# Attention and a gated layer on one core: the last output tile cut at column 448 instead of 384

## The chip, the cores and the metric

The kernel runs on one core of a Trainium2 chip. The metric is the device time of one execution in microseconds; lower is better. Three runs of the kernel before gave 247.82, 247.95 and 248.65 us, median 247.95.

Engines are named as in the profile: PE is the matrix engine (TensorE), with PEld its weight loads; DVE the vector engine; ACT the scalar engine; POOL and SP the two others, which here only move data. A q behind a name (SPq, ACTq) means the instructions with which that engine starts a DMA or waits.

## The reference

For each of 8 batches and 8 heads (576 tokens, head size 64) two attentions follow each other: 32 packed queries p attend to k and v, and the packed result serves as keys and values for q. The heads are joined to rows of 512, and a two-layer network with a gated activation follows:

```python
def sm_attn(qq, kk, vv):
    s = scale * np.matmul(qq, kk.transpose(0, 1, 3, 2))
    a = np.exp(s - np.max(s, axis=-1, keepdims=True))
    return np.matmul(a / (np.sum(a, axis=-1, keepdims=True) + 1e-09), vv)

p_packed = sm_attn(p, k, v)
x = sm_attn(q, p_packed, p_packed)       # heads joined: 4608 x 512
h = x @ w_in                             # 4608 x 2048
g = np.where(h >= 1, h, np.where(h <= -1, 0.0, (h + 1) ** 2 / 4))
out = g @ w_out                          # 4608 x 512, float32
```

## The kernel before

The attention of a batch yields a matrix M (packed values already multiplied by w_in) and the weights A; `hidden_tile` multiplies the two into a hidden tile h of 128 features by 576 tokens (L588), and ACT and DVE apply the activation (L593 to L603) and leave hT, the hidden values by feature, in bf16. Two batches make a pair of 1152 tokens, nine output tiles of 128 tokens each. `out_tile` sums one such tile: 16 matmuls (KF = 16 blocks of 128 features), each with a block of hT as the stationary operand (128 x 128) and the 512 columns of w_out as the moving one (L647), into a PSUM tile o of 128 x 512. Then a copy (L329, called from `done` at L660) brings o to SBUF as ob, on ACT or DVE, and a DMA (L662) stores ob's rows to DRAM.

What order the work takes is fixed before the program runs: `Plan` holds a list of tasks with costs, due times (keys) and dependencies, simulates the engines with those costs, and emits each task at the moment at which it would start. The costs of a task of `out_tile` are C["o"] for a matmul of 512 columns, scaled by the piece's width, and C["oba"] or C["obd"] for the copy on ACT or DVE.

Only the very last tile of the program (pair 3, tile 8; `end` at L634) is treated differently: its columns are cut into two pieces (L638). All 16 matmuls of the first piece run, then all 16 of the second. The first piece has a tile from the pool for outputs (tag o); the second, `j` = 1, has one from the pool of wide tiles (`room`, L641, tag w). So each of the 16 blocks of hT is loaded as weights twice. The first piece is copied by DVE and stored from SP's queue; the second is copied by ACT and stored from ACT's queue (L662 and L683). The last tile's 128 tokens all lie in batch 7 and in one half of it, so each piece is stored by one DMA of 128 rows (`out_rows`, L617 to L622). A row in DRAM holds one token's columns of the piece: 384 float32 (1536 bytes) and 128 float32 (512 bytes).

Behind the last store stands the program's end (L757): SP waits for the completion of every outstanding store, one after the other, then the engines meet in a barrier.

Of the kernel before, what the change touches and what calls it, by code (L numbers as in the profile page):

```python
# [36 lines left out]
class Plan:  # L37
# [15 lines left out]
    def add(self, engines, cost, key, deps, fn, takes=None, readers=0, frees=None, mode=None, slack=None, after=0.0,  # L53
            holds=0.0):
        engines = (engines,) if isinstance(engines, str) else engines
        t = Task(engines, cost if isinstance(cost, dict) else {e: cost for e in engines}, key, deps, fn, takes, readers,
                 frees, mode, slack, after, holds)
        t.seq = len(self.tasks)
        self.tasks.append(t)
        return t  # L60
# [129 lines left out]
def kernel(  # L190
# [18 lines left out]
    d_model, d_ff = moe_w_in.shape  # L209
# [36 lines left out]
    def wide(shape, dtype, name):  # L246
        return psW.tile(shape, dtype, tag="w", name=name)
# [76 lines left out]
    def both(fns, cost_a, cost_d, key, deps, **kw):  # L324

        return add((DVE, ACT), {ACT: cost_a, DVE: cost_d}, key, deps, fns, **kw)

    def copy(out_, in_):
        return lambda eng: nc.vector.tensor_copy(out_, in_) if eng == DVE else nc.scalar.copy(out_, in_)  # L329
# [283 lines left out]
    def out_rows(pr, i):  # L613
        res, t = [], i * P
        while t < (i + 1) * P:
            b, x, e, r = 2 * pr + t // S, t % S // HALF, t % HALF // TP, t % TP
            if b == B - 1:  # L617
                r = t % HALF
                n = min(HALF - r, (i + 1) * P - t)
                res.append((t - i * P, n, out[b * S:(b + 1) * S].rearrange("(r x) d -> x r d", x=X)[x, r:r + n]))  # L620
                t += n
                continue  # L622
            n = min(TP - r, (i + 1) * P - t)
            res.append((t - i * P, n, out[b * S:(b + 1) * S].rearrange("(p c) d -> c p d", c=NC)[X * e + x, r:r + n]))
            t += n
        return res
# [3 lines left out]
    def out_tile(pr, i):  # L630
        box, prev = {}, []
        bs = range(2 * pr + i * P // S, 2 * pr + ((i + 1) * P - 1) // S + 1)

        end = 2 * pr + 2 == B and i + 1 == NT  # L634

        cuts = [CUT, KF] if pr == 0 and i < PARTS else [KF]

        pieces = [slice(0, 3 * d_model // 4), slice(3 * d_model // 4, d_model)] if end else [slice(0, d_model)]  # L638

        def room(j, part=0):  # L640
            box["o", j, part] = wide([P, d_model], f32, "o2") if j else psO.tile([P, d_model], f32, tag="o", name="o")  # L641

        def step(fi, j, cs):
            part = int(fi >= cuts[0])
            if not j and (fi == 0 or fi in cuts):
                room(0, part)
            nc.tensor.matmul(box["o", j, part][:, :cs.stop - cs.start], hT[:, fi, i * P:(i + 1) * P], w_out_sb[:, fi, cs],  # L647
                             start=(fi == 0 or fi in cuts), stop=(fi + 1 in cuts))

        def kept(eng):  # L650
            box["part"] = att.tile([P, d_model], f32, tag="part", name="part", bufs=PARTS)
            copy(box["part"], box["o", 0, 0])(eng)

        def done(eng, j, cs):
            ob, o = ops.tile([P, d_model], f32, tag="ob", name="ob"), box["o", j, len(cuts) - 1]
            ob, o = [v[:, :cs.stop - cs.start] for v in (ob, o)]
            if len(cuts) > 1:
                nc.vector.tensor_tensor(ob, o, box["part"], ALU.add)
            else:
                copy(ob, o)(eng)  # L660
            for a, n, dst in out_rows(pr, i):
                (nc.scalar if j else nc.sync).dma_start(dst[:, cs], ob[a:a + n])  # L662
        for j, cs in enumerate(pieces):
            cost = C["o"] * (cs.stop - cs.start) / d_model
            if j:
                prev = prev + [add(PE, 0.0, 100 + pr * NT + i, prev, lambda: room(1), takes="W", readers=1)]
                owner = prev[-1]
            for fi in range(KF):
                t = add(PE, cost, 100 + pr * NT + i, [wrote[b, fi] for b in bs] + prev + [L["out", fi // 4]],
                        lambda fi=fi, j=j, cs=cs: step(fi, j, cs), mode=0, takes="O" if not j and (fi == 0 or fi in cuts) else None,  # L670
                        readers=1, slack=C["slack"])
                if not j:
                    step_of[pr, i, fi] = t
                prev = [t]
                if t.takes:
                    owner = t
                if fi + 1 in cuts[:-1]:
                    first = both(kept, C["oba"], C["obd"], b_key(pr, i), prev, frees=owner)
            fn = lambda eng, j=j, cs=cs: done(eng, j, cs)
            if len(cuts) > 1:  # L680
                add(DVE, C["obd"], b_key(pr, i), prev + [first], fn, frees=owner, takes="ob", holds=C["out"])
            elif end:
                add(ACT if j else DVE, C["oba"] if j else C["obd"], b_key(pr, i), prev, fn,  # L683
                    frees=owner, takes="ob", holds=C["out"])
            else:
                both(fn, C["oba"], C["obd"], b_key(pr, i), prev, frees=owner, takes="ob", holds=C["out"])

    def b_key(pr, i):
        return -0.5 if pr else C["bk"] - 1.0
# [19 lines left out]
    for b in range(B):  # L709
        if b + 2 < B:  # L710
            add_load("k", b + 2, deps=K[b, "kt"])
            add_load("q", b + 2, deps=K[b, "qt"])
            add_load("v", b + 2, deps=K[b, "pk"])
        K[b, "h"] = [hidden_tile(b, fi, b + fi / KF) for fi in range(KF)]
        if b == 0:

            for f in range(1, NF):
                K[b, "M"][f].deps.append(K[b, "h"][4 * f - 4])
            attention(1, keys[1])
            add_pT(PB, 4, 0.9, [L["p", PB]], False)  # L720
            add_p(4, B)
            add_pT(4, B, C["p4"], [L["p", 4]], False)
        if b % 2 == 1:
            for i in range(NT):
                out_tile(b // 2, i)
        if 0 < b < B - 1:
            attention(b + 1, keys[b + 1])
# [34 lines left out]
```

## Time and profile before

| | us |
|---|---|
| median of three runs | 247.95 |
| the profiled execution, its own time | 247.93 |
| its span, first to last instruction | 246.2 |
| PE busy in it | 237.6 |
| ACT busy | 189.5 |
| DVE busy | 180.0 |

The time of the profiled execution is 1.7 us above its span, for what lies before the first and after the last instruction. The granted TensorE clock was 1.000 throughout. A matmul's record is longer than the pace at which matmuls follow each other, since they overlap in the array: the pace is read from a run of equal ones, divided by their number. A DMA's row gives the time from its issue to its landing, that is, to when its completion is signalled.

### The profile page before, as it was taken

To read this page: it belongs to the slowest core of one execution; us is meant where nothing else is said; L and a number is where in the kernel's file an instruction comes from. 1 tells how busy PE (TensorE), PEld (TensorE's weight loads), DVE (VectorE), ACT (ScalarE), POOL (GpSimd) and SP (SyncE) were. 2 spreads that over 40 slices of the span, in tenths; PEclk is the share of its full clock that TensorE was granted. 3 is DMA by queue.
4 is the path that set the end of the run, shared out by engine and by line. 5 is a ranking of instruction groups with operands and counts; after the bars stand their busy time and mean duration, and the time that the engine had idled before them with its cause. 6 is when DMAs were issued, how large, how long until landed. Compare 5 with 4: busy or idle time off the path is not lost.

```text
span 246.2 us, 5439 instructions
## 1 busy us (share of the span) xinstructions
PE 237.6 (97%) x2188; PEld 139.1 (57%) x2224; DVE 180.0 (73%) x308; ACT 189.5 (77%) x306; POOL 30.0 (12%) x45
## 2 busy tenths in 40 slices
PE   8999999999999999999999999999999999999994
PEld 2645566467645764476446654666466555654443
DVE  4457998978974988798866996698788787985000
ACT  2376898999978989789877897899888887984110
POOL 8632333212001201011101100000000000000000
PEclk9999999999999999999999999999999999999999
DMA  7999999999999999999987991444522121122222
GB/s 103 197 207 205 206 204 201 205 251 223 190 189 165 252 189 199 181 139 173 183 140 140 174 203 45 91 93 92 120 55 55 43 45 43 43 44 78 52 85 85
DMA packets 54777, 34.37 MB, mean 140 GB/s; under 512 B 27488, under 2 KB 50272, under 8 KB 54752
## 3 DMA queue, kind: packets, MB, share of 16 engines
q0 software_dynamic: 24688, 18.55, 51.0%
q1 hardware_dynamic: 29920, 15.41, 30.3%
q8 instruction: 17, 0.28, 0.4%
q10 hardware_dynamic: 144, 0.07, 0.1%
q14 instruction: 8, 0.07, 0.1%
HBM read 37.22 MB, written 9.44 MB: 190 GB/s over the span
## 4 chain that ended last, share of the span: by engine, by line
PE 83%; DMA 11%; issue 2%; ACT 2%; DVE 1%; POOL 0%; ACTq 0%; POOLq 0%
PE o L647 49%; PE h L588 22%; DMA k<-in_k_dram 7%; PE mp L533 3%; DMA q<-in_q_dram 3%; PE pk L433 2%; PE sp L413 2%; PE tp L386 2%; PE sm L482 2%; DMA qT<-q 2%; ACT x L593 1%; PE s L467 1%; PE pk L439 1%; DVE M L329 1%; POOL k L268 0%
## 5 line engine op out<-in xcount | busy, mean ns | idle before, releaser
L647 PE MATMUL o<-w_out_sb,hT 128*128 128x512 bf16 (+2 forms) x559 | 135.8, 373 | 1.9 <-issue 1.0
L603 DVE SCALAR_TENSOR_TENSOR hT<-x 128x576 bf16<-128x576 f32 x128 | 94.4, 755 | 7.5 <-ACT x L600 4.8
L593 ACT ACTIVATE x<-h 128x576 f32<-128x576 f32 x128 | 77.0, 651 | 12.2 <-PE h L588 9.9
L647 PEld LDWEIGHTS <-hT 128*128 128x128 bf16 x592 | 55.3, 98 | 54.8 <-issue 5.0
L588 PE MATMUL h<-A,M 128*128 128x288 bf16 x512 | 74.8, 286 | 0.3
L588 PEld LDWEIGHTS <-M 128*128 128x128 bf16 x512 | 49.3, 98 | 21.2 <-ACT M L329 0.6
L598 DVE TENSOR_SCALAR x<-x 128x576 f32<-128x576 f32 x81 | 37.0, 457 | 12.5 <-ACT x L593 12.4
L600 ACT ACTIVATE x<-x 128x576 f32<-128x576 f32 x47 | 31.4, 682 | 0.3
L329 ACT COPY ob<-o 128x512 f32<-128x512 f32 (+1 forms) x22 | 12.6, 571 | 21.8 <-PE o L647 21.7
L329 DVE COPY ob<-o 128x512 f32<-128x512 f32 (+1 forms) x11 | 7.5, 678 | 21.1 <-DMA out_dram<-ob 16.7
L329 ACT CAST M<-mp 128x1024 bf16<-128x1024 f32 x19 | 18.7, 1014 | 0.9 <-PE mp L533 0.7
L329 DVE CAST M<-mp 128x1024 bf16<-128x1024 f32 x13 | 15.7, 1220 | 4.9 <-PE mp L533 4.9
L416 ACT ACTIVATE ex<-sp 96x768 bf16<-96x768 f32 x16 | 12.8, 801 | 4.5 <-PE sp L413 4.5
L502 DVE SCALAR_TENSOR_TENSOR A<-eT,rs,rc 128x576 bf16<-128x576 bf16 (+1 forms) x15 | 11.5, 775 | 5.4 <-ACT rc L492 5.4
L731 PE MATMUL o<-zeros 128*128 128x512 bf16 (+1 forms) x45 | 13.0, 425 | 1.3 <-DVE zeros L256 1.2
L477 ACT ACTIVATE eT<-s,rs 128x576 bf16<-128x576 f32 (+1 forms) x17 | 11.5, 712 | 3.3 <-PE s L467 3.2
L268 POOL DMA_DIRECT2D k<-in_k_dram x10 | 7.6, 758 | 51.2 <-DMA kT<-k 28.3
L268 POOL DMA_DIRECT2D q<-in_q_dram x10 | 7.3, 735 | 40.6 <-DMA qT<-q 25.3
L487 ACT ACTIVATE ln<-sm 128x576 f32<-128x576 f32 (+1 forms) x17 | 10.6, 624 | 1.8 <-PE sm L482 1.6
L492 ACT ACTIVATE rc<-ln 128x576 f32<-128x576 f32 (+1 forms) x17 | 11.0, 654 | 0.4
L533 PE MATMUL mp<-w_in_sb,ppT 64*32 64x512 bf16 x256 | 10.6, 380 | 0.1
L413 PEld LDWEIGHTS <-kT 128*128 128x128 bf16 x192 | 7.8, 98 | 2.1
(51 smaller groups left out, 123.1 us busy)
## 6 DMA issues: line engine op xcount, KB each, us to landing
out_dram<-ob SPq DMA_DIRECT2D x23, 192.0 KB, 2.5
v<-in_v_dram POOLq DMA_DIRECT2D x7, 576.0 KB, 18.2
k<-in_k_dram POOLq DMA_DIRECT2D x6, 576.0 KB, 12.5
q<-in_q_dram POOLq DMA_DIRECT2D x6, 576.0 KB, 12.8
out_dram<-ob SPq DMA_DIRECT2D x22, 128.0 KB, 2.6
w_in_sb<-in_moe_w_in_dram POOLq DMA_DIRECT2D x4, 512.0 KB, 13.5
w_out_sb<-in_moe_w_out_dram POOLq DMA_DIRECT2D x4, 512.0 KB, 17.2
out_dram<-ob SPq DMA_DIRECT2D x22, 64.0 KB, 2.1
```

The lines of the kernel that those rows point to most:

```text
L268: nc.gpsimd.dma_start(tok[nm, b][:, hs].rearrange("p h c d -> p h (c d)"), SRC[nm][b, hs].rearrange("h (p c) d -> p h (c d)", c=NC))
L329: return lambda eng: nc.vector.tensor_copy(out_, in_) if eng == DVE else nc.scalar.copy(out_, in_)
L413: nc.tensor.matmul(o[:, :, a], kT()[:, i, w:w + P], pT[:, b, h], start=True, stop=True)
L416: nc.scalar.activation(ex()[:, :, i].rearrange("p e x a n -> p e (x a n)"), box["sp"], AF.Exp, scale=scale)
L533: nc.tensor.matmul(mp[a * NP:(a + 1) * NP, g], pp_of(y, h), w_in_sb[y * D:(y + 1) * D, h // 2, f * FW:(f + 1) * FW], start=True, stop=True)
L588: nc.tensor.matmul(h[:, hf, :HALF], T[b, "M"][:, g, fi * P:(fi + 1) * P], T[b, "A"][:, g, hf], start=(g == 0), stop=(g == G - 1))
L593: nc.scalar.activation(box["x"], box["h"][:, :, :HALF], AF.Prelu, bias=-1.0, alpha=0.5)
L598: nc.vector.tensor_scalar(x, x, 1.0, 0.0, ALU.add, ALU.max)
L600: nc.scalar.activation(x, x, AF.Relu, bias=1.0)
L603: nc.vector.scalar_tensor_tensor(hT[:, fi, col:col + S].rearrange("p (a t) -> p a t", a=2), box["x"], 1.0, box["x"], ALU.min, ALU.mult)
L647: nc.tensor.matmul(box["o", j, part][:, :cs.stop - cs.start], hT[:, fi, i * P:(i + 1) * P], w_out_sb[:, fi, cs], start=(fi == 0 or fi in c ...
L731: plan.run(lambda w: nc.tensor.matmul(o[:, :w], zeros[:, :P], zeros[:, :w], start=True, stop=True))
```

## The change

The cut of the last tile moves from column 384 (three quarters) to column 448 (seven eighths):

```diff
-        pieces = [slice(0, 3 * d_model // 4), slice(3 * d_model // 4, d_model)] if end else [slice(0, d_model)]
+        pieces = [slice(0, 7 * d_model // 8), slice(7 * d_model // 8, d_model)] if end else [slice(0, d_model)]
```

All else follows from this line through `step` and `done`. On PE, 16 matmuls of 384 columns become 448 wide and 16 of 128 columns become 64 wide. DVE's copy goes from 128 x 384 to 128 x 448, ACT's from 128 x 128 to 128 x 64. SP's store of the tile grows from 192 KB in rows of 1536 bytes to 224 KB in rows of 1792 bytes; ACT's shrinks from 64 KB in rows of 512 bytes to 32 KB in rows of 256 bytes. The two programs, once built, hold the same number of instructions in the same order on each engine; only these sizes differ. Engines, queues, PSUM tiles and buffers of the two pieces stay as they are.

## The prediction

> **What bounds the kernel now.** I read the page's head and chain first, then the last microseconds by the timeline, then SP's own waits and the DMA view of the tail.
>
> ```profile
> span 246.2 us, 5439 instructions
> PE 237.6 (97%) x2188; PEld 139.1 (57%) x2224; DVE 180.0 (73%) x308; ACT 189.5 (77%) x306; POOL 30.0 (12%) x45
> PE 83%; DMA 11%; issue 2%; ACT 2%; DVE 1%; POOL 0%; ACTq 0%; POOLq 0%
> ```
>
> TensorE is busy for 97% of the span and 83% of the chain of waits. The edit touches neither its amount of arithmetic nor anything ahead of the last output tile, so only the end of the program is in question. The timeline there (start, length, engine, line):
>
> ```profile
> 241.23 1.54 PE L647 MATMUL o<-w_out_sb,hT 128*128 128x384 bf16 x19
> 241.92 0.56 DVE L329 COPY ob<-o 128x384 f32<-128x384 f32 x1 [16.70 <-DMA out_dram<-ob]
> 242.50 0.34 SPq L662 DMA_DIRECT2D out_dram<-ob  x1
> 242.85 0.27 ACT L329 COPY ob<-o 128x128 f32<-128x128 f32 x1 [2.95 <-PE o L647]
> 243.15 0.37 ACTq L662 DMA_DIRECT2D out_dram<-ob  x1
> ```
>
> TensorE ends at 241.23 + 1.54 = 242.77. There are two branches: first piece, DVE copy, SP's queue; second piece, ACT copy, ACT's queue. Which branch ends last is told by the landings and by SP, which at the program's end waits for one transfer after the other. The DMA view of 242.5 to 244.9 (40 slices of 0.06 us):
>
> ```profile
> GB/s 0 0 0 0 0 0 0 0 0 0 0 0 0 0 205 333 410 384 384 410 358 282 333 154 26 51 188 273 299 188 86 9 0 0 0 0 0 0 0 0
> out_dram<-ob SPq DMA_DIRECT2D x1, 192.0 KB, 2.0
> out_dram<-ob ACTq DMA_DIRECT2D x1, 64.0 KB, 1.7
> ```
>
> SP's transfer lands at 242.50 + 2.0 = 244.5, ACT's at 243.15 + 1.7 = 244.85. SP's own waits, first in 242.5 to 244.6 and then in 244.6 to 246.2, agree:
>
> ```profile
> SPq L757 <- DMA out_dram<-ob: 1.5, 1, 1.5
> SPq L757 <- DMA out_dram<-ob: 0.3, 1, 0.3
> ```
>
> After the first landing SP still waits 0.3 us for the second. So **the ACT branch, the second piece, ends last, by about 0.35 us**; from 244.85 to the span's end at 246.2 stand only 1.3 us of closing barriers (L757), which the edit leaves alone. The first piece has 0.35 us of slack, and that is the budget the edit spends.
>
> **The change part by part.** The built programs hold the same instructions in the same order on every engine; sizes alone differ. The planner's order is therefore untouched, and no semaphore wait, queue or buffer is new.
>
> *TensorE.* The pace of matmuls by width, from the chain between 182.9 and 184.3:
>
> ```profile
> 182.95 0.35 PE sp L413 x12
> 183.30 0.43 PE o L647 x2
> 183.73 0.49 PE h L588 x4
> ```
>
> The page's shapes are 64 columns for sp, 512 for o and 288 for h. That is 29.2, 215 and 122.5 ns each, which one line fits: 2.6 ns + 0.415 ns per column (122.1 at 288). By it a 384-column matmul takes 162.0 ns, 448 takes 188.5, 128 takes 55.7 and 64 takes 29.2. Before: 16 x (162.0 + 55.7) = 3.48 us. After: 16 x (188.5 + 29.2) = 3.48 us. TensorE still ends at 242.77; only the border between the pieces moves, by 16 x 26.5 ns = **0.43 us later**.
>
> The rule that speaks against this is in the Trainium skill, "TensorE: Matmul & The Clock Gate", section "Back-to-back issue gap": a stream of weight load and matmul pairs is said to sustain some 81 ns at 128 columns, since the weight load needs its share. By it the narrow piece would not get shorter with its columns, TensorE would end up to 0.43 us later, and the second branch, 0.05 us shorter by its copy, would land up to 0.38 us later: a sum of +0.4 us in place of the one below. This trace disagrees, since the sp row has 29.2 ns at 64 columns with a weight load for each matmul, of the same 128 x 128 shape:
>
> ```profile
> L413 PE MATMUL sp<-pT,kT 128*128 128x64 bf16 x192 | 8.3, 193 | 0.1
> L413 PEld LDWEIGHTS <-kT 128*128 128x128 bf16 x192 | 7.8, 98 | 2.1
> ```
>
> I take the row; the price if the loads did bind at the pace of 128 columns is 16 x 26.5 ns = 0.43 us.
>
> *The copies.* Grouped by form:
>
> ```profile
> L329 DVE COPY ob<-o 128x512 f32<-128x512 f32 x10 | 6.9, 690 | 4.4 <-PE o L647 4.3
> L329 DVE COPY ob<-o 128x384 f32<-128x384 f32 x1 | 0.6, 559 | 16.7 <-DMA out_dram<-ob 16.7
> L329 ACT COPY ob<-o 128x512 f32<-128x512 f32 x21 | 12.3, 586 | 18.8 <-PE o L647 18.7
> L329 ACT COPY ob<-o 128x128 f32<-128x128 f32 x1 | 0.3, 267 | 3.0 <-PE o L647 3.0
> ```
>
> DVE: (690 - 559)/128 = 1.02 ns per column, so 448 columns take 0.625 us. It starts 0.43 later, at 242.35, and ends at 242.97; SP issued 0.02 us behind the copy's end before, so it issues at **243.00** instead of 242.50. ACT: (586 - 267)/384 = 0.83 ns per column, so 64 columns take 0.214 us, 0.05 less; it starts at 242.85 as before and its DMA goes out at **243.10** instead of 243.15. Nothing is queued behind either instruction except the closing barrier.
>
> *The transfers.* ACT's branch alone would now land at 243.10 + 1.7 = 244.8, 0.05 earlier. SP's branch carries 224 KB. The tile before it, all 256 KB on SP's queue, in the DMA views of 239.9 to 240.0 (its issue) and of 240.7 to 241.7 (its packets):
>
> ```profile
> out_dram<-ob SPq DMA_DIRECT2D x1, 256.0 KB, 2.0
> q1 hardware_dynamic: 144, 0.26, 70.3%
> ```
>
> 192 KB and 256 KB both land after 2.0 us when alone, so 224 KB does too: 243.00 + 2.0 = 245.0. That is the lower bound, +0.15 us over 244.85. But it is no longer alone. Before, the issues were 0.65 us apart and the bursts stood behind each other (the two humps in the GB/s row: the first slice at 243.34, 0.84 after SP's issue, and the dip at 243.94). Now they are 0.10 apart and share the 16 engines. The work of each, from the view of 243.3 to 244.4 (1.1 us):
>
> ```profile
> q1 hardware_dynamic: 144, 0.20, 51.3%
> q10 hardware_dynamic: 144, 0.07, 21.5%
> ```
>
> 192 KB cost each engine 0.51 x 1.1 = 0.56 us, and 256 KB cost 0.70 x 1.0 = 0.70, so 224 KB cost 0.63. The small transfer cost 0.24 us for 8 rows of 512 bytes per engine, 30 ns a row; 1536-byte rows cost 70 ns (0.56/8), so a row of 256 bytes is estimated at 30 - 256 x 40/1024 = 20 ns, and 8 of them at 0.16 us. Together 0.79 us of work, whichever queue is served first. From SP's issue: 0.84 to the first packet, 0.79 of work, and 0.43 from the last packet (244.42 in the GB/s row) to the landing at 244.85; the same sum for 192 KB alone gives 242.50 + 0.84 + 0.56 + 0.43 = 244.33 where 244.5 was measured, so 0.15 is added for engines that start unevenly. 243.00 + 0.84 + 0.79 + 0.43 + 0.15 = **245.2**, against 244.85.
>
> *Sum.* The pieces of TensorE 0; the end of the last transfer +0.35 us (bounds: +0.15 where the small transfer costs the large one nothing, -0.05 where the large one were hidden altogether). The profiled execution took 247.93 us with a span of 246.15; 247.93 + 0.35 = **248.3 us**. Its time stands 0.02 under the median of the three runs, 247.95. So +0.14%, which is below the 0.3% (0.74 us) that a measurement of this kernel can tell from no change.
>
> **The rivals.**
>
> *Short rows are slow to store* (slower). The second piece's rows into DRAM shrink from 512 to 256 bytes, and no transfer of the trace stores rows as short as that; nothing stands behind it to hide a delay. It decides from a landing 0.8 us later than the 1.7 that 512-byte rows take (243.10 + 2.5 = 245.6, which is 244.85 + 0.74). If each row is first read and then written, the worst is one more such trip: 243.10 + 3.4 = 246.5, +1.65 us, 249.6; half of it gives +0.8 us, 248.75. Against it: from 2048 over 1536 to 512 bytes the engine time per row falls evenly, with no step. The Trainium skill, "DMA: Bandwidth & Descriptors", section "Specifications", has this rule: below 512 bytes the engine does a read-modify-write. No row of this trace shows it. Chance 0.20, around 249.0.
>
> *Two queues in flight hinder each other* (slower) by more than their summed work. For it: SP's pairs of smaller transfers on one queue landed later than a single one:
>
> ```profile
> out_dram<-ob SPq DMA_DIRECT2D x23, 192.0 KB, 2.5
> out_dram<-ob SPq DMA_DIRECT2D x22, 128.0 KB, 2.6
> ```
>
> A landing after 2.6 us instead of 2.0 gives 245.6 without and 245.8 with the shared work: +0.75 to +0.9, 248.7 to 248.85. It decides from 2.6. Against it: those medians come mostly from the middle of the program, where loads run. Chance 0.17.
>
> *The first piece is still hidden*: its landing takes under 1.85 us and ACT's 0.05 us counts, so 247.9. The 2.0 of both larger transfers speaks against it. Chance 0.05, no change.
>
> *Faster by over 0.74 us* would need both landings by 244.1, 1.0 us behind ACT's issue, while no transfer in the tail took under 1.7. Chance 0.04, around 247.1.
>
> **How the numbers follow.** The forecast, +0.1 to +0.7 us (248.05 to 248.65), has 0.54. With the hidden case, within 0.3% is 0.59; the two slow cases make 0.37, and 0.04 is faster. The range runs from 247.8 (hidden, less a tenth of run-to-run scatter) to 249.2, which takes in the second slow case and over half of the first.
>
> **What would show it.** Right: DVE's copy of 128x448 starts near 242.35 and takes 0.62; SP's issue is near 243.0 and ACT's near 243.1; one hump of DMA traffic in place of two; SP's longer wait ends on its own transfer near 245.2, and the wait behind it is nearly nothing. The weight-load step is wrong if TensorE ends after 242.9; the short-row step if ACT's landing takes over 2.0 us; the sharing step if SP's transfer lands at 2.0 (too dear) or beyond 2.4 (too cheap). The whole is wrong if the time leaves the tail: any shift ahead of 239 us is outside this account.

## The result, and the profile after

The changed kernel took 248.51 us (median of 15 runs, 248.24 to 249.12) against 248.22 us (15 runs, 247.78 to 248.65): ratio 1.0018, 95% interval 1.0011 to 1.0025. That is +0.44 us (0.27 to 0.62; the medians alone lie 0.29 us apart, inside that interval): resolved by this many runs, and inside the 0.3% that counts as no change. The forecast was +0.35 us.

The page of the changed kernel, its head and its chain of waits by engine:

```profile
span 246.7 us, 5475 instructions
PE 240.7 (98%) x2224; PEld 138.7 (56%) x2224; DVE 180.0 (73%) x308; ACT 189.4 (77%) x306; POOL 29.8 (12%) x45
PE 88%; DMA 9%; issue 1%; POOL 0%; ACT 0%; ACTq 0%; POOLq 0%
```

The 3 us more of PE are no more work: the profile of the kernel before holds 36 matmul records fewer (2188 against 2224), although the two programs have the same instructions and both profiles hold 2224 weight loads. DVE and ACT are busy as before. The end of the program in the timeline (start, length, engine, line):

```profile
241.31 1.57 PE L647 MATMUL o<-w_out_sb,hT 128*128 128x448 bf16 x21
242.45 0.63 DVE L329 COPY ob<-o 128x448 f32<-128x448 f32 x1 [17.12 <-PE o L647]
242.96 0.21 ACT L329 COPY ob<-o 128x64 f32<-128x64 f32 x1 [2.95 <-PE o L647]
243.10 0.35 SPq L662 DMA_DIRECT2D out_dram<-ob  x1
243.20 0.37 ACTq L662 DMA_DIRECT2D out_dram<-ob  x1
```

TensorE ends at 241.31 + 1.57 = 242.88, 0.11 us later than before (the granted clock between 241 and 242.9 us is 1.00 in both). In the thirteen other profiles of this study that moment lies between 242.7 and 243.5, and the two profiles of the changed kernel have 242.88 and 243.46: what runs ahead of the last tile scatters by more than the whole effect. So all later times are counted **from TensorE's end**. DVE's copy starts 0.43 before it (0.85 in the kernel before: 242.77 - 241.92), SP's issue comes 0.22 behind it instead of 0.27 ahead, ACT's 0.32 behind it instead of 0.38.

The DMA view of 242.5 to 245.5, in 40 slices of 0.075 us:

```profile
GB/s 0 0 0 0 0 0 0 0 0 0 0 0 0 0 0 0 0 0 0 167 358 358 382 382 382 382 382 267 195 178 62 0 0 0 0 0 0 0 0 0
q1 hardware_dynamic: 144, 0.23, 21.0%
q10 hardware_dynamic: 144, 0.03, 5.4%
out_dram<-ob SPq DMA_DIRECT2D x1, 224.0 KB, 2.1
out_dram<-ob ACTq DMA_DIRECT2D x1, 32.0 KB, 2.2
```

The two humps with a dip between them are now one. The engines' work is 0.21 x 3 = 0.63 us for the large store and 0.054 x 3 = 0.16 us for the small one, as estimated. But the small one, with half of its bytes, lands 2.2 us after its issue where it took 1.7. Its row minus TensorE's end: 243.20 + 2.2 - 242.88 = 2.5, against 244.85 - 242.77 = 2.1 before.

To the hundredth of a microsecond, from the trace's records of the profiles of all runs, from TensorE's end (packets are those of the DMA engines that carry rows; landing is where SP's wait for that store ends; the labels are those of the experiments below):

| kernel | SP issue | ACT issue | SP's packets | ACT's packets | SP landed | ACT landed |
|---|---|---|---|---|---|---|
| before | -0.27 | 0.38 | 0.57 to 1.26 | 1.26 to 1.62 | 1.70 | **2.07** |
| changed | 0.22 | 0.32 | 1.07 to 1.83 | 1.68 to 1.95 | 2.37 | **2.55** |
| after_again | 0.22 | 0.32 | 1.07 to 1.84 | 1.67 to 1.96 | 2.38 | **2.55** |
| e1_rows512 | 0.22 | 0.28 | 1.06 to 1.76 | 1.58 to 1.96 | 2.21 | **2.45** |
| e2_one_store | 0.22 | none | 1.06 to 1.81 | none | **2.24** | none |
| e3_short_alone | -0.27 | 0.38 | 0.56 to 1.26 | 1.26 to 1.54 | 1.68 | **1.96** |
| e4_shorter_alone | -0.27 | 0.38 | 0.57 to 1.27 | 1.27 to 1.49 | 1.69 | **1.88** |
| e5_half_large | 0.22 | 0.32 | 1.06 to 1.59 | 1.42 to 1.71 | 2.08 | **2.27** |
| e6_rows128 | 0.23 | 0.32 | 1.07 to 1.83 | 1.68 to 1.91 | 2.28 | **2.46** |
| e7_held_back | 0.22 | 0.63 | 1.06 to 1.83 | 1.66 to 1.95 | 2.37 | **2.54** |
| e8_same_large | 0.22 | 0.32 | 1.06 to 1.76 | 1.60 to 1.87 | 2.21 | **2.38** |
| cut320 | -0.76 | 0.43 | 0.07 to 0.67 | 1.30 to 1.74 | 1.17 | **2.28** |
| cut416 | -0.02 | 0.35 | 0.82 to 1.58 | 1.42 to 1.76 | 2.03 | **2.24** |
| three_pieces | 0.01 | 0.32 | 0.84 to 1.29 | 1.21 to 1.47 | 1.84 | **2.01** |

For three_pieces SP's columns are its second store. The two profiles of the changed kernel agree to 0.01 us in every column, and the same large store shows the same times to 0.02 us in the kernel before, e3_short_alone and e4_shorter_alone. So differences of 0.05 us in this table mean something, as far as these repeats show, while the ratios below have intervals of about 0.0009 (0.2 us) to either side. The last landing moved from 2.07 to 2.55: **+0.47 us** (differences are taken before rounding), which agrees with the measured +0.44 (0.27 to 0.62).

### The profile page after: what moved, and what is told of

It reads as the page before. It is cut to its first block, busy times and chain, and to the rows that moved or that the text cites. A ratio compares the mean times of both kernels' runs of the same rounds, so it can differ in the third digit from the quotient of the medians.

```text
span 246.7 us, 5475 instructions
## 1 busy us (share of the span) xinstructions
PE 240.7 (98%) x2224; PEld 138.7 (56%) x2224; DVE 180.0 (73%) x308; ACT 189.4 (77%) x306; POOL 29.8 (12%) x45
## 4 chain that ended last, share of the span: by engine, by line
PE 88%; DMA 9%; issue 1%; POOL 0%; ACT 0%; ACTq 0%; POOLq 0%
PE o L647 51%; PE h L588 24%; DMA k<-in_k_dram 7%; PE mp L533 3%; DMA q<-in_q_dram 3%; PE pk L433 2%; PE sp L413 2%; PE tp L386 2%; PE sm L482 1%; PE s L467 1%; PE pk L439 1%; POOL k L268 0%; PE tpp L343 0%; ACT ob L329 0%; ACTq L329 0%
## 5 line engine op out<-in xcount | busy, mean ns | idle before, releaser
L647 PE MATMUL o<-w_out_sb,hT 128*128 128x512 bf16 (+2 forms) x592 | 143.0, 374 | 0.0
L731 PE MATMUL o<-zeros 128*128 128x512 bf16 (+1 forms) x48 | 14.0, 427 | 1.2 <-DVE zeros L256 1.2
```

What stands on the lines that cost most here:

```text
L731: plan.run(lambda w: nc.tensor.matmul(o[:, :w], zeros[:, :P], zeros[:, :w], start=True, stop=True))
```

## The experiments

Each run gives a ratio to the kernel before, and a row of the table.

**Does the small store's row length matter beside the large one? (e1_rows512)** The pieces as in the change, the stores as before it:

```diff
-            ob, o = ops.tile([P, d_model], f32, tag="ob", name="ob"), box["o", j, len(cuts) - 1]
-            ob, o = [v[:, :cs.stop - cs.start] for v in (ob, o)]
+            ob, o = box.get("ob"), box["o", j, len(cuts) - 1]
+            if ob is None:
+                ob = box["ob"] = ops.tile([P, d_model], f32, tag="ob", name="ob")
+            whole, ob, o = ob, ob[:, cs], o[:, :cs.stop - cs.start]
+            ss = cs if not end else slice(384, d_model) if j else slice(0, 384)
...
-                (nc.scalar if j else nc.sync).dma_start(dst[:, cs], ob[a:a + n])
+                (nc.scalar if j else nc.sync).dma_start(dst[:, ss], whole[a:a + n, ss])
```

> The pieces are cut at 448, but stored as before the change: columns 0 to 383 from SP's queue, 384 to 511 (rows of 512 bytes) from ACT's queue once both copies are done. Issues near 243.0 (SP) and 243.1 (ACT) from the span's start, as in the changed kernel. Theory S (two bursts share the engines behind a late issue, 0.8 us of work together, whatever the row size): the last landing is as late as in the changed kernel, +0.35 to +0.45 us over the kernel before, ratio 1.0014 to 1.0018. Theory R (rows of 256 bytes take longer from the last packet to the landing, 0.59 against 0.45 us): the last landing is 0.15 us sooner, +0.2 to +0.3 us, ratio 1.0008 to 1.0012, and ACT's store shows 0.45 us from its last packet to its landing.

Ratio 1.0015 (1.0006 to 1.0024), last landing 2.45. Most of the delay is there with 512-byte rows: +0.37 of the +0.47 us. The remaining 0.1 us spoke for R, and the next runs took it up.

**The large store without the small one (e2_one_store):**

```diff
-                (nc.scalar if j else nc.sync).dma_start(dst[:, cs], ob[a:a + n])
+                if not j:
+                    nc.sync.dma_start(dst[:, cs], ob[a:a + n])
```

> The changed kernel without the second store (columns 448 to 511 of the last 128 tokens aren't written). SP's 224 KB are alone. The lower bound of the prediction: issue at 243.0, landing 2.0 us later, 0.15 us over the end of the kernel before, ratio 1.0006 (1.0003 to 1.0009). S and R both expect this; if instead the ratio stays at 1.0018, neither sharing nor short rows matter and the late issue of SP alone is worth 0.4 us.

Ratio 0.9998 (0.9989 to 1.0006), whose interval just reaches the 1.0006 expected. The DMA view has its landing:

```profile
out_dram<-ob SPq DMA_DIRECT2D x1, 224.0 KB, 2.0
```

From TensorE's end it landed at 2.24, 0.17 us behind the last landing of the kernel before. The lateness of the large store alone is worth +0.17 of the +0.47 us; the small store beside it makes the other 0.31.

**Short rows with the engines free (e3_short_alone, e4_shorter_alone).** The kernel before, with less of the second piece stored:

```diff
-                (nc.scalar if j else nc.sync).dma_start(dst[:, cs], ob[a:a + n])
+                if j:
+                    nc.scalar.dma_start(dst[:, d_model - 64:], ob[a:a + n, cs.stop - cs.start - 64:])
+                else:
+                    nc.sync.dma_start(dst[:, cs], ob[a:a + n])
```

> The kernel before (cut at 384, ACT copies 128 columns), but ACT stores only the last 64 of them, in rows of 256 bytes (columns 384 to 447 of the last 128 tokens aren't written). Its store is issued 0.65 us after SP's and meets no other transfer. S: the 0.08 us of work saved shows, landing 1.6 us after the issue, ratio 0.9996 to 1.0. R: landing 1.75 to 1.85 us after the issue though half the bytes move, +0.05 to +0.15 us, ratio 1.0002 to 1.0006.

The same with 32 for 64:

> As the kernel before, but ACT stores only its last 32 columns, in rows of 128 bytes (columns 384 to 479 of the last 128 tokens aren't written). S: landing 1.55 us after the issue, ratio 0.9994 to 1.0. R: at least as late as with 256 bytes, 1.75 to 1.9 us after the issue, ratio 1.0002 to 1.0008.

Ratios 0.9999 (0.9990 to 1.0007) and 0.9995 (0.9986 to 1.0005). ACT's store in the DMA view, first with 256-byte rows:

```profile
out_dram<-ob ACTq DMA_DIRECT2D x1, 32.0 KB, 1.6
```

and then with 128-byte rows:

```profile
out_dram<-ob ACTq DMA_DIRECT2D x1, 16.0 KB, 1.5
```

512-byte rows took 1.7. The store gets shorter with its bytes, and from the last packet to the landing it took 0.45 us with 512-byte rows, 0.42 with 256, 0.39 with 128: R falls here. A row costs an engine 29, 18 and 13 ns. The Trainium skill, "DMA: Bandwidth & Descriptors", section "Specifications", has a read-modify-write below 512 bytes; if these stores did one, it cost no time that these runs show.

**Short rows next to another store (e8_same_large, e6_rows128).** The changed kernel with SP's store cut to columns 0 to 383, so that it differs from e1_rows512 in the second store (and in that ACT need not wait for DVE):

```diff
-                (nc.scalar if j else nc.sync).dma_start(dst[:, cs], ob[a:a + n])
+                if end and not j:
+                    nc.sync.dma_start(dst[:, :384], ob[a:a + n, :384])
+                else:
+                    (nc.scalar if j else nc.sync).dma_start(dst[:, cs], ob[a:a + n])
```

> The changed kernel with SP storing columns 0 to 383 only (192 KB; 384 to 447 of the last 128 tokens aren't written) and ACT 64 columns in rows of 256 bytes. Against the run with the same 192 KB beside 512-byte rows (last landing 2.45 behind TensorE's end) only the second store differs. Q alone: 0.08 us less work, landing near 2.35. R (rows of 256 bytes are slow to be confirmed, but only next to another store): 0.1 us from the last packet to the landing more than with 512-byte rows, landing at 2.42 to 2.47.

Ratio 1.0013 (1.0004 to 1.0022), landing 2.38: 0.06 us sooner than with 512-byte rows, between the two expectations and nearer to Q's. And with ACT storing its last 32 columns only:

```diff
-                (nc.scalar if j else nc.sync).dma_start(dst[:, cs], ob[a:a + n])
+                if j:
+                    nc.scalar.dma_start(dst[:, d_model - 32:], ob[a:a + n, 32:])
+                else:
+                    nc.sync.dma_start(dst[:, cs], ob[a:a + n])
```

> The changed kernel with ACT storing its last 32 columns only, rows of 128 bytes (columns 448 to 479 of the last 128 tokens aren't written). Q alone: 0.05 us less work than with 256-byte rows, landing near 2.5. R next to another store: from the last packet to the landing 0.6 us or more, landing at 2.5 to 2.6, no gain for half the bytes.

Ratio 1.0014 (1.0005 to 1.0023), landing 2.46, sooner than either expectation. From the last packet to the landing it took 0.55 us against the changed kernel's 0.59: shorter rows, shorter wait. So R falls beside another store too; the 0.1 us between e1_rows512 and the changed kernel is not a matter of 256-byte rows. It goes with the size of SP's store: e8_same_large and the changed kernel differ in that alone (192 against 224 KB), and the last landing is at 2.38 in the one and 2.55 in the other.

**Who waits for whom (e5_half_large, e7_held_back).** The changed kernel with half of SP's store:

```diff
-                (nc.scalar if j else nc.sync).dma_start(dst[:, cs], ob[a:a + n])
+                if end and not j:
+                    nc.sync.dma_start(dst[:, :cs.stop // 2], ob[a:a + n, :cs.stop // 2])
+                else:
+                    (nc.scalar if j else nc.sync).dma_start(dst[:, cs], ob[a:a + n])
```

> The changed kernel with only the first half of SP's last store (columns 0 to 223, 112 KB; columns 224 to 447 of the last 128 tokens aren't written); copies, issues and ACT's store are as in the changed kernel. All times from TensorE's end. Theory Q (each DMA engine works off its share of SP's store before it begins ACT's, so ACT's store waits for the large one): SP's packets last from 1.07 to 1.45, ACT's begin by 1.35 instead of 1.68 and the last landing is at 2.05 to 2.1 instead of 2.55, 0.45 us sooner than the changed kernel, ratio to the kernel before 0.9998 to 1.0002. Rival L (two stores in flight simply take 2.2 us each, whatever their size): ACT's landing stays 2.2 us after its issue, at 2.5, ratio 1.0015 to 1.002.

Ratio 1.0002 (0.9990 to 1.0014). ACT's store is the same one, issued at the same moment, and landed 0.28 us sooner (2.27 against 2.55), since its packets began at 1.42 instead of 1.68. That is 0.17 less than Q expected: the packets came 0.07 late, and took 0.56 to land instead of 0.45. L falls. The row of ACT's store in the DMA view:

```profile
out_dram<-ob ACTq DMA_DIRECT2D x1, 32.0 KB, 1.9
```

The other way round, ACT's store held back by three spare copies:

```diff
+                if j:
+                    spare = att.tile([P, 3, 64], f32, tag="spare", name="spare", bufs=1)
+                    for i_ in range(3):
+                        nc.scalar.copy(spare[:, i_], o)
                 copy(ob, o)(eng)
```

> The changed kernel with ACT copying the second piece three times to a spare tile first, so that its store is issued about 0.6 us later, near 0.93 behind TensorE's end instead of 0.32. Q: the store then meets engines that are just done with SP's (1.83) and takes the 1.58 us that it took alone: landing near 2.5, no later than the changed kernel's 2.55; ratio to the kernel before 1.0016 to 1.0019, SP's own landing at 2.24 as with one store. Rival L (a store issued near another takes 2.2 us anyway): landing at 3.1, 0.6 us later, ratio 1.004.

The copies held it back by 0.30 us only, half of what was meant (the three take 0.44 us together, overlapping). The timeline:

```profile
242.91 0.44 ACT L663 COPY spare<-o 128x64 f32<-128x64 f32 x3 [2.91 <-PE o L647]
243.10 0.35 SPq L666 DMA_DIRECT2D out_dram<-ob  x1
243.23 0.24 ACT L329 COPY ob<-o 128x64 f32<-128x64 f32 x1
243.50 0.37 ACTq L666 DMA_DIRECT2D out_dram<-ob  x1
```

and the landings in the DMA view:

```profile
out_dram<-ob SPq DMA_DIRECT2D x1, 224.0 KB, 2.1
out_dram<-ob ACTq DMA_DIRECT2D x1, 32.0 KB, 1.9
```

ACT's issue is at 243.50 instead of 243.20 and its landing takes 1.9 instead of 2.2: the 0.3 us are gone without trace. Packets begin at 1.66 and land at 2.54, as in the changed kernel (1.68 and 2.55). So the store had been waiting for the engines: issued 0.30 us later, it started and ended at the same moments. The ratio, 1.0008 (0.9999 to 1.0017), lies lower than the 1.0016 to 1.0019 expected, with the interval reaching it; in this profile the closing barriers behind the last landing took 1.2 us instead of 1.3.

**Other cuts.** `pieces` cut at 416 and at 320:

> The cut at column 416, half way between the two kernels. Q: SP's issue is 0.02 us before TensorE's end, its 208 KB occupy the engines from 0.82 to 1.55, ACT's 48 KB could start at 1.24 but begin near 1.42 and end near 1.76; last landing at 2.2, 0.15 us over the kernel before, ratio 1.0006. Rival H (the stores don't hinder each other; only the issues count): both land at 1.97 to 2.0, 0.08 us sooner than before, ratio 0.9997.

> The cut at column 320, on the other side of the kernel before. Q: SP's store is through by 0.9 behind TensorE's end, ACT's copy of 192 columns takes 0.32 us, its 96 KB are issued near 0.43, begin at 1.32 unhindered, end near 1.75 and land near 2.2, 0.1 us over the kernel before: ratio 1.0004 (1.0001 to 1.0007).

Ratios 1.0010 (1.0001 to 1.0020) and 1.0006 (0.9997 to 1.0015); last landings 2.24 and 2.28, +0.17 and +0.21 us. H falls with the first: SP's packets end at 1.58, and ACT's, which could start at 0.35 + 0.89 = 1.24, 0.89 us behind their issue as in the kernels cut at 384 (0.88) and three_pieces (0.89), start at 1.42. At 320 nothing is in the way (1.30 is 0.87 behind the issue), but the piece is larger, its copy and its packets take longer, and 0.54 us pass from the last packet to the landing. On both sides of 384 the last landing is later, though the ratio of the cut at 320 leaves no change possible.

**Three pieces**, the narrow one last, ACT's, and the columns ahead of it in two stores from SP's queue:

```diff
-        pieces = [slice(0, 3 * d_model // 4), slice(3 * d_model // 4, d_model)] if end else [slice(0, d_model)]
+        pieces = [slice(0, 256), slice(256, 448), slice(448, d_model)] if end else [slice(0, d_model)]
...
-                (nc.scalar if j else nc.sync).dma_start(dst[:, cs], ob[a:a + n])
+                (nc.scalar if j == 2 else nc.sync).dma_start(dst[:, cs], ob[a:a + n])
...
-                prev = prev + [add(PE, 0.0, 100 + pr * NT + i, prev, lambda: room(1), takes="W", readers=1)]
+                prev = prev + [add(PE, 0.0, 100 + pr * NT + i, prev, lambda j=j: room(j), takes="W", readers=1)]
...
-                add(ACT if j else DVE, C["oba"] if j else C["obd"], b_key(pr, i), prev, fn,
+                add(ACT if j == 2 else DVE, C["oba"] if j == 2 else C["obd"], b_key(pr, i), prev, fn,
```

> Three pieces: 0 to 255 and 256 to 447 by DVE and SP's queue, 448 to 511 by ACT and its queue. Q: the first 128 KB are issued 1.2 us before TensorE's end and are through by 0.2; the 96 KB are issued at -0.05 and occupy the engines from 0.8 to 1.2; ACT's 32 KB begin at 1.21 unhindered and land at 1.93, 0.14 us sooner than in the kernel before, less 0.04 us for 16 more matmuls: ratio 0.9996 (0.9993 to 1.0). If landings are slow whenever another store is in flight (L), the last is at 2.5, ratio 1.002.

Ratio 0.9996 (0.9988 to 1.0005). The same 64 columns, copied and issued by ACT at the same moment as in the changed kernel (0.32), now begin at 1.21, 0.89 behind the issue, and land at 2.01 instead of 2.55. What made the cut at 448 slow is not the narrow piece but the large store before it. Against the kernel before it is 0.06 us sooner by landing, less than the 0.14 expected (0.54 us from the last packet to the landing again); no run tells it from that kernel.

**The changed kernel once more:**

> The changed kernel once more, on the chip of the runs beside it: ratio 1.0018 (1.0011 to 1.0025), last landing 2.4 to 2.55 us behind TensorE's end. How far this profile's landings are from the first one's tells their scatter.

Ratio 1.0017 (1.0007 to 1.0026), landing 2.55.

## Why the prediction came out right, and where it did not

**TensorE and the copies.** Right. The border between the pieces moved by 0.42 us (0.43 forecast; 16 x 26.5 ns is 0.42), DVE's copy took 626 ns (625), ACT's 212 (214). The narrow matmuls were not held by their weight loads: the group of sixteen is 0.6 us busy with 193 ns each, so (0.6 - 0.19)/15 = 0.03 us apart, and their records start 29 ns apart, as forecast (the lines are grouped by form):

```profile
L647 PE MATMUL o<-w_out_sb,hT 128*128 128x64 bf16 x16 | 0.6, 193 | 0.0
L329 DVE COPY ob<-o 128x448 f32<-128x448 f32 x1 | 0.6, 626 | 17.1 <-PE o L647 17.1
L329 ACT COPY ob<-o 128x64 f32<-128x64 f32 x1 | 0.2, 212 | 3.0 <-PE o L647 3.0
```

**The issues.** Right: 0.22 and 0.32 us behind TensorE's end, forecast 243.00 and 243.10 less 242.77, 0.23 and 0.33.

**The late large store.** Right: +0.15 forecast as the lower bound, +0.17 shown by the landing with the small store taken away; the ratio of that run, 0.9998, is too coarse to show it.

**The two stores on the same engines.** Right in kind: 0.79 us of work in one hump, and a last packet at 1.95 where 245.2 less 0.43 of landing less 242.77 gives 2.0. The prediction left open which queue is served first. The table answers it: ACT's first packet comes 8 of SP's rows after SP's first one. With 1792-byte rows of 78 ns, 1.07 + 8 x 0.078 = 1.69 against 1.68 measured; with half of them (47 ns), 1.06 + 0.38 = 1.44 against 1.42; at the cut at 416 (76 ns), 0.82 + 0.61 = 1.43 against 1.42. Eight rows are an engine's whole share of a store of 128 rows, so each engine finishes SP's share before it starts ACT's. The trace's records say so more directly: a store's 144 packets are its 128 rows and 16 of 4 bytes that close it, nine to each of 16 engines. In the changed kernel, its repeat, e5, e6, e7, e8 and the cut at 416 ACT's first packet begins within 0.01 us of the end of the first 4-byte packet of SP's (in e1_rows512 it comes 0.03 us ahead of it). The Trainium skill, "DMA: Bandwidth & Descriptors", section "Queues, rings and completion order", has the engines change between queues only after a packet of some 9 to 17 descriptors. If a descriptor there is what the trace lists as a packet, one a row, then eight rows and a completion are within one, and these runs agree.

So the step that was wrong is which branch ends last. The prediction had SP's transfer last, at 245.2, and the wait behind it nearly nothing; ACT's landed last, 0.17 us behind SP's. The branch that had bounded the kernel bounds it still, now because it queues behind the one that had slack. The forecast came near all the same because its sum holds the work of both stores, whichever is served first, and so did not depend on the branch it named.

**The size.** +0.35 forecast, +0.47 by landing. The term that was too small is the landing itself: 0.43 us from the last packet, taken from a store that was alone, where 0.59 passed in the changed kernel (from the unrounded times). That is +0.16; packets that ended 0.05 sooner than forecast take part of it back.

**The rivals.** Short rows: refuted at the size it named, alone and beside another store. The prediction's sign for it, a landing of ACT's store after more than 2.0 us, did appear (2.2), but e3_short_alone and e7_held_back show that it was a sign of waiting for the engines. Two queues that hinder each other by more than their work: the extra wait for the landing is of that kind, but 0.1 to 0.2 us, not the 0.4 to 0.6 that it needed: from the last packet to the landing ACT's 256-byte rows took 0.42 us alone and 0.59 in the changed kernel, and SP's 224 KB 0.42 alone (e2_one_store) and 0.54. Hidden first piece, and faster: no.

**Open** is what stretches the time from the last packet to the landing. For ACT's store it was 0.39 to 0.45 us in the three kernels cut at 384, and 0.48 to 0.59 in all others, which include two whose packets nothing stood in the way of (cut320 and three_pieces, 0.54 each). Row length, size and overlap each fail to order these values. The two stores of cut320, far apart in time, took 0.50 (SP's, rows of 1280 bytes) and 0.54 (ACT's, 768 bytes), against 0.42 to 0.45 for 1536 bytes in the kernels cut at 384 and 0.45 for 512, so rows of middling length may land later by themselves; three_pieces, with 256-byte rows, would still stand outside that, and no run tests it. No difference between chips shows behind it, although the runs were spread over several: the store of the tile before, 256 KB in every kernel, was signalled 0.34 to 0.35 us after its last packet in all fourteen profiles.

## What to carry to other kernels

Where two branches at a program's end share the DMA engines, as here, slack on one of them is not free: a store issued later by its slack can come to stand in front of the other's. Find the moment at which the last store's packets could start (here its issue plus 0.89 us) and let the store ahead of it be through by then. In the kernel before, SP's packets ended at 1.26, just as ACT's began. A cut to the right of 384 makes ACT's store wait; the one to the left, at 320, has a larger last piece that is issued later and moves longer. Where the stretch ahead scatters by 0.3 us and more, count from the last event that both kernels share: here the tail then told differences of 0.05 us that 15 runs don't.

## What was not expected of the hardware

Stores of 256-byte and 128-byte rows into DRAM, alone, landed 1.6 and 1.5 us after their issue, sooner than 512-byte rows (1.7). A second store issued 0.30 us later landed no later. The two profiles of one kernel had the same tail to 0.01 us though TensorE's end lay 0.58 us apart in them.
